# Four edits to the opening of a float32 attention and two-MLP kernel: order of the weight conversion, form of the shift pass, place of the second block's state products, order of the attention's PSUM banks

## The chip, the cores and the metric

The kernel runs on one core of a Trainium2 chip. The metric is the time of one execution on the device, in microseconds (us), the median of several runs. TensorE is called PE here (its weight loads PEld), VectorE DVE, ScalarE ACT, GpSimd POOL; SP is the engine that issues nearly all DMAs.

## The reference

Inputs are `x` (8 x 8 heads x 512 x 64), `state` (8 x 8 x 32 x 64) and two MLPs' weights, which arrive as float64.

```
scores = x @ state^T / 8 ; a = softmax(scores) ; xread = a @ state
scores2 = state @ x^T / 8 ; a2 = softmax(scores2) ; sread = a2 @ x
z = heads joined of [xread, sread]              # 8 x 544 rows of 512
h = z @ w1_in (512 x 2048) ; g = max(h,0) + alpha*min(h,0) ; y = g @ w1_out (2048 x 512)
h2 = y @ w2_in ; g2 = h2 - tanh(h2) ; out = g2 @ w2_out
```

## The kernel before

**Precision.** Each float32 operand is split into a high part (rounded to fp32r, PE's input format) and a low part (the rest); a product is three matmuls, `TERMS` (line 29): high x high, high x low, low x high.

**Weight conversion.** The float64 words of the first MLP's weights become high and low parts in 32 jobs (list `jobs`, line 127): job (f, 0) makes slice f (128 columns) of `w1_in`, called an input slice here, job (f, 1) slice f (128 rows) of `w1_out`, an output slice. A job goes through a pipeline, one stage a tick: `conv_load` (a DMA of 512 KB on SP's queue), `conv_a` (ACT, absolute value), `conv_b` (DVE, `high_word`: a clamp, line 115, and the shift pass, line 117, which shifts left by 3 and masks), `conv_s` (DVE, `sign_word`, line 120; ACT, low word), `conv_c` (ACT copy of the high part; POOL add, line 167), `conv_d` (POOL subtract, lines 173 and 176). `high_word` also serves the second MLP's weights, 32 times, in `combine` (tiles named `c_m`), in the middle of the span.

**Order of the work.** An order written out by hand. The MLP's work is a list of visits (block, slice f): block 0 with slices 0 to 7, block 1 with all 16, block 0 with 8 to 15, then the other blocks. A visit issues `emit_h` (the input product, line 605: 12 matmuls in block 0, 6 in block 1), `act_a` (ACT line 612, DVE 613, ACT 614), `act_b` (DVE 618, low part of the activations) and `emit_o` of the visit before (the output product, line 633, 12 matmuls). Between them are five places, early, gap, mid, late and end; `at(block, slice, place, step)` hangs a step there. `halves` hangs the conversion's ticks, two a visit in block 0's first half and one in block 1, but two in block 1's slices 2 to 4. Every engine does its instructions in the order of issue, so a step that waits holds up all that is behind it on its engine.

**Attention.** The next block's attention is done in steps `s0` to `s6` between the MLP's products. Its PSUM tiles come from the pool `ps_a`, two banks used by turns: a new tile waits until the tile two back has been read. The transposes of the state (`state_turn`, line 361) and the state products (below) take banks of the same pool.

**State products.** From block 1 on the attention's read is not computed first: `project_one(b, q, g, p)` (line 403) multiplies the state with 512 columns q of `w1_in` (line 410, three matmuls), for a pair of heads p of half g, and `emit_h` uses the result `PW` with the attention weights. Rows 0 to 63 and 64 to 127 of one product belong to two blocks (1 and 2 here). Before, high and low part go to a staging tile (lines 413 and 414; for block 1 free parts of a weight tile first, the attention's buffers later), from there to DRAM (line 416), and `load_parts` (line 418) brings block 1's rows back into `PW` (line 423; in the first two quarters slots of the tile `wo`, later buffers `raw`).

**First loads.** `load_x` and `load_state` fetch the first block's first half on SP's queue and its second half on ACT's (`queue`, line 310).

Of the kernel before, what the change touches and what calls it, by code (L numbers as in the profile page):

```python
# [12 lines left out]
F32 = mybir.dt.float32  # L13
F32R = mybir.dt.float32r
I32 = mybir.dt.int32
# [7 lines left out]
P = 128  # L23
# [12 lines left out]
def attention_and_two_mlps(ctx, tc, x, state, w1_in, w1_out, alpha, w2_in, w2_out, out):  # L36
# [30 lines left out]
    ident = const.tile([P, P], F32, name="ident")  # L67
    mask = const.tile([P, GH], F32, name="mask")
    par = const.tile([P, 2], F32, name="par")
    alpha_sb = const.tile([P, NF], F32, name="alpha_sb")  # L70

    sign = const.tile([P, NF], F32, name="sign")
# [3 lines left out]
    def setup():  # L76
        make_identity(nc, ident)
        nc.vector.memset(mask, 0.0)
        nc.vector.memset(par, 0.0)
        for h in range(GH):  # L80
            nc.vector.memset(mask[h * NS:(h + 1) * NS, h:h + 1], 1.0)
            nc.vector.memset(par[h * NS:(h + 1) * NS, h % 2:h % 2 + 1], 1.0)
        nc.sync.dma_start(out=alpha_sb, in_=alpha.rearrange("(f p) -> p f", p=P))
# [30 lines left out]
    def high_word(m):  # L114
        nc.vector.tensor_scalar(m.bitcast(F32), m.bitcast(F32), HIGH_MAX, HIGH_MIN,
                                op0=ALU.min, op1=ALU.max)
        nc.vector.tensor_scalar(m, m, 3, LOW30, op0=ALU.logical_shift_left, op1=ALU.bitwise_and)

    def sign_word(m, r):
        nc.vector.scalar_tensor_tensor(m, r[:, :, 1], SIGN_TOP, m,  # L120
# [3 lines left out]
        nc.scalar.activation(q, r[:, :, 0].bitcast(U32), AF.Copy, scale=2.0**-29)  # L124


    jobs = [(f, half) for f in range(NF // 2) for half in range(2)]
    jobs += [(f, 0) for f in range(8, 12)] + [(8, 1)] + [(f, 0) for f in range(12, 16)] + [(f, 1) for f in range(9, NF)]
    raws, words, low, loaded = {}, {}, {}, set()

    def conv_load(k):
# [175 lines left out]

    xraw, SG = {}, {}

    def queue(b, g):  # L310
        return nc.scalar if (b, g) == (0, 1) else nc.sync

    def load_state(b, g, tag="sg"):
        sg = work.tile([P, D], F32, tag=tag, name=f"{tag}{b}_{g}", bufs=4)
        queue(b, g).dma_start(out=sg, in_=state[b, g * GH:(g + 1) * GH].rearrange("h n d -> (h n) d"))
        SG[(b, g) if tag == "sg" else (b, g, 0)] = sg

    def load_x(b, g):
        if b < 2:
            load_state(b, g)  # L320
        if b == 0:
            if g == 0:
                xraw[b] = w_outs.tile([P, 2 * NC * GH * D], F32, tag="wo", name="xr0")
            n = NC * GH * D
            t = xraw[b][:, g * n:(g + 1) * n].rearrange("p (c h d) -> p c h d", c=NC, h=GH)
        else:
            t = work.tile([P, NC, GH, D], F32, tag="xr", name=f"xr{b}_{g}")
        for h in range(GH):
            queue(b, g).dma_start(out=t[:, :, h, :],
                              in_=x[b, g * GH + h].rearrange("(p c) d -> p c d", c=NC))  # L330
        xraw[b, g] = t

# [40 lines left out]
            nc.vector.tensor_tensor(o[:, 1, sel, :], src, o[:, 0, sel, :].bitcast(F32), op=ALU.subtract)  # L373

    def parts_tile(b, q, g):
        if b == 1 and q < 2:
            open_wo(NF // FQ - 1)
            t = WO[NF // FQ - 1][:, :, 2 * q + g, :]
        else:
            t = work.tile([P, 2, DM], F32R, tag="raw", name="pw", bufs=4)  # L380
        PW[b, q, g] = [t[:, 0], t[:, 1]]
        return t
# [5 lines left out]
    def staged(b):  # L388


        if b > 1:
            return (work.tile([P, DM], F32R, tag="cm", name="ph", bufs=3),
                    work.tile([P, DM], F32R, tag="cq", name="pl", bufs=3))
        k = n_staged[0]
        n_staged[0] += 1
        if k < 8:
            open_wi(NF // FQ - 1)
            return tuple(WI[NF // FQ - 1][:, i, k % NCC, :] for i in range(2))
        return tuple(work.tile([P, DM], F32R, tag=t, name="pe", bufs=1) for t in (("e2", "e2t"), ("sc", "at"))[k % 2])
# [3 lines left out]
    def project_one(b, q, g, p):  # L403


        both = b + 1 < B
        cols, d = (slice(2 * p, 2 * p + 2), slice(0, P)) if both else (slice(3 * p, 3 * p + 1), slice(p * HP, (p + 1) * HP))
        ps = ps_a.tile([P, DM], F32, tag="a", name="ps_p")[:P if both else HP]
        for k, (i, j) in enumerate(TERMS):
            nc.tensor.matmul(ps, lhsT=SN[b, g][:, i, cols, :].rearrange("p k m -> p (k m)"),  # L410
                             rhs=WI[q][:, j, g * NP + p, :], start=(k == 0), stop=(k == 2))
        hi, lo = staged(b)
        nc.scalar.copy(hi[d], ps)
        nc.vector.tensor_tensor(lo[d], ps, hi[d].bitcast(F32), op=ALU.subtract)
        for k, t in enumerate((hi, lo)):
            nc.sync.dma_start(out=pw_dram[b, q, g][p, k, d], in_=t[d].bitcast(F32))

# [614 lines left out]
    def at(i, f, when, *todo):  # L1032
        plan.setdefault((i, f, when), []).extend(todo)

    def timetable(i, a, c):

        if i == 0:
            when = dict(s0=(2, "late"), s1=(3, "early"), s2=(3, "late"), s2t=(3, "end"), s2b=(3, "end"), s3=(3, "end"),
                        s3x=(4, "gap"), s3b=(4, "late"), s4=(4, "end"), s4m=(4, "end"), s4t=(4, "end"), s4b=(5, "gap"),
                        s5=(5, "early"), s6=6)  # L1040
            then = dict(s0=(5, "late"), s1=(6, "early"), s2=6, s2t=(6, "late"), s2b=(6, "late"), s3=(6, "late"),
                        s3x=(6, "end"), s3b=7, s4=(7, "early"), s4m=(7, "early"), s4t=(7, "gap"), s4b=7, s5=(7, "late"),
                        s6=(NF, "late"))
        else:
            def table(first):
                return dict(s0=first, s1=first + 1, s2=first + 2, s2t=(first + 3, "gap"), s2b=first + 3,
                            s3=(first + 4, "gap"), s3x=first + 4, s3b=(first + 4, "late"), s4=(first + 5, "gap"),
                            s4m=first + 5, s4t=(first + 6, "gap"), s4b=(first + 6, "late"), s5=first + 6,
                            s6=(first + 7, "late"))
            start = 7 if i + 2 < B else 5  # L1050
            when, then = (table(0), table(start)) if i > 1 else (table(9), table(8 + NF))
        for g, table in ((a, when), (c, then)):
            for name, w in table.items():
                f, place = w if isinstance(w, tuple) else (w, "mid")

                if f >= NF:
                    j, f = (1, f - NF) if i == 0 else (0, f - NF + (NF // 2 if g is a else 0))
                    at(j, f, place, getattr(g, name))
                else:
                    at(i, f, place, getattr(g, name))  # L1060

    with tc.manual_schedule():
# [15 lines left out]

        for f in range(NF // 2):
            halves(0, f, "early", "gap")  # L1080
        for f in range(11):
            if f in (2, 3, 4):
                halves(1, f, "early", "gap", "mid", "end")
            else:
                halves(1, f, "gap", "end")
        at(0, 0, "gap", a.s2b)
        at(0, 0, "late", c.s2b)
        at(0, 1, "mid", a.s3b, c.s3b)
        at(0, 2, "mid", a.s5)
        at(0, 2, "late", c.s5)  # L1090
        at(0, 3, "mid", a.s6, c.s6)
        a = attention(1, 0)
        turns = [(0, 1, 0, (0, "mid"), (1, "late")), (0, 2, 0, (1, "late"), (2, "early")),
                 (0, 1, 1, (3, "mid"), (4, "early")), (0, 2, 1, (3, "late"), (4, "late"))]
        for i in (2, 4, 6):
            turns += [(i, i + 1, 0, (0, "early"), (0, "late")), (i, i + 1, 1, (2, "late"), (3, "late"))]
            if i + 2 < B:
# [13 lines left out]
            at(i, f, "early", partial(state_mask, b, g, True))  # L1111
            at(i, f, "end", partial(state_turn, b, g, scores=False))
        todo = [(1, q, g) for q in range(NF // FQ) for g in range(NG)]
        places = [(0, 4), (0, 5), (1, 0), (1, 1), (1, 3), (1, 4), (1, 6), (1, 7)]
        todo += [(b, q, g) for b in (3, 5, 7) for g in range(NG) for q in range(NF // FQ)]
        places += [(0, f) for f in range(8, NF)] + [(2, f) for f in range(NF)]
        for (b, q, g), (i, f) in zip(todo, places):
# [1 line left out]
            at(i, f, "late", partial(project_one, b, q, g, 1))  # L1119
        for k in range(2 * NF // FQ):  # L1120
            at(*((0, 9 + 2 * k) if k < 4 else (2, 2 * k - 7)), "end", partial(save_w_in, k // 2, k % 2))
        for q, (i, f, place) in enumerate(((0, 7, "early"), (1, 2, "late"), (1, 6, "early"), (1, 9, "early"))):
            at(i, f, place, partial(load_parts, 1, q))
        at(0, 10, "late", load_half_sum)
        for i, (blk, n) in enumerate(seq):
            if 1 < blk < B:
# [4 lines left out]
        for i, (blk, n) in enumerate(seq):  # L1131
            if i + 1 < B:
                timetable(i, a, attention(i + 1, 1))
                if i + 2 < B:
                    a = attention(i + 2, 0)
                    for j, f in (((1, 2), (1, 4)), ((0, 9), (0, 15)))[i] if i < 2 else ((i, 6), (i, 13)):
                        at(j, f, "late", load_next_x)
            if i + 1 < len(seq) and seq[i + 1][0] == B:
                nn = seq[i + 1][1]
                at(i, 13, "mid", partial(load_reads, nn))  # L1140
                for cc in range(NCC):
                    at(i, *((NF - 1, "early") if cc > 1 else (14, "mid")), partial(split_reads, cc, nn))
# [184 lines left out]
```

## Time and profile before

| | us |
|---|---|
| median of 3 runs | 1507.78 (1504.39 to 1513.72) |
| the profiled execution, whole | 1510.44 |
| its span, first to last instruction | 1508.6 |
| PE busy in the span | 1422.1 (94%) |
| DVE busy | 991.6 (66%) |
| ACT busy | 729.7 (48%) |
| POOL busy | 532.1 (35%) |
| granted PE clock, mean | 0.982 |

The profile is of one execution. Busy time is the union of an engine's instructions. The whole time has 1.8 us beside the span. The granted clock is the share of PE's full speed, 2.4 GHz, that was given; its other level is 1.2 GHz. PE is nearly always busy from about 180 us on; in the first 180 us it is not, and there DVE is.

### The profile page before, as it was taken

What the parts mean: (1) busy time and instruction counts of PE and PEld (TensorE: products, weight loads), DVE (VectorE), ACT (ScalarE), POOL (GpSimd) and SP (SyncE); (2) the same over time, 40 slices, a digit from 0 to 9 for tenths busy, and PEclk for the clock granted to TensorE, in tenths of its full rate; (3) what the DMA queues carried; (4) which work ended last, traced back from release to release, by engine and by line L of the source; (5) the groups of instructions that cost most, each with busy time, mean ns of one, the idle gap of its engine ahead of it and who ended that gap; (6) DMA issues with size and microseconds to landing.
All of it is one profiled execution on the core that took longest, in us unless ns stands there. A gap on an engine that the chain in (4) does not pass through costs nothing. (4 is left out here: it accounts for less than half of the span.)

```text
span 1508.6 us, 22873 instructions
## 1 busy us (share of the span) xinstructions
PE 1422.1 (94%) x8188; PEld 1192.1 (79%) x8188; DVE 991.6 (66%) x1430; ACT 729.7 (48%) x1322; POOL 532.1 (35%) x414
## 2 busy tenths in 40 slices
PE   5868899999899999999999899999999999999998
PEld 2656687677677677778887787887988999999998
DVE  6879855556577667676345555646347798788874
ACT  3656543444565555555334444545345444444443
POOL 2545400000254444445200222212016486666662
PEclk9998999999999999999999999999999999999999
DMA  5458628795688587749864666272795834444321
GB/s 150 137 163 253 206 80 286 268 300 129 188 213 238 156 247 225 239 158 298 237 209 151 253 202 247 103 272 105 276 346 205 324 133 141 133 141 140 133 85 36
DMA packets 230979, 294.41 MB, mean 195 GB/s; under 512 B 57809, under 2 KB 133585, under 8 KB 229841
## 3 DMA queue, kind: packets, MB, share of 16 engines
q1 hardware_dynamic: 228608, 292.39, 60.2%
q8 instruction: 64, 1.05, 0.3%
q10 hardware_dynamic: 2256, 0.56, 0.2%
q14 instruction: 51, 0.41, 0.1%
HBM read 170.73 MB, written 122.16 MB: 194 GB/s over the span
## 5 line engine op out<-in xcount | busy, mean ns | idle before, releaser
L633 PE MATMUL acc<-g,wo 128*128 128x512 f32 (+1 forms) x1728 | 416.2, 388 | 20.8 <-ACT g L614 11.8
L633 PEld LDWEIGHTS acc<-g,wo 128*128 128x128 f32 x1728 | 312.2, 191 | 104.0 <-ACT g L614 16.6
L1001 PE MATMUL ps_m<-wp,s 128*128 128x256 f32 x2856 | 343.5, 283 | 2.1 <-ACT e L984 2.0
L1001 PEld LDWEIGHTS ps_m<-wp,s 128*128 128x128 f32 x2856 | 342.5, 191 | 3.2 <-ACT e L984 2.2
L820 PE MATMUL ps_m<-x,ch 128*128 128x512 f32 x1344 | 312.7, 394 | 8.6 <-DVE c L837 4.5
L820 PEld LDWEIGHTS ps_m<-x,ch 128*128 128x128 f32 x1344 | 251.7, 188 | 69.0 <-DVE c L837 6.5
L946 DVE TENSOR_TENSOR s<-gt,s 128x512 fp32r<-128x512 f32 (+1 forms) x216 | 220.5, 1072 | 45.4 <-ACT s L962 44.4
L613 DVE SCALAR_TENSOR_TENSOR ps_h<-ps_h,sign,t 128x512 f32<-128x512 f32 (+1 forms) x144 | 104.7, 727 | 144.9 <-ACT t L612 144.4
L614 ACT ACTIVATE g<-ps_h,sign 128x512 fp32r<-128x512 f32 (+1 forms) x144 | 95.8, 666 | 160.5 <-DVE ps_h L613 160.5
L962 ACT CAST s<-gt 128x512 fp32r<-128x512 f32 (+1 forms) x216 | 120.3, 597 | 90.9 <-PE ps_m L1001 37.5
L605 PE MATMUL ps_h<-x,pw 128*128 128x512 f32 x624 | 162.7, 396 | 0.9 <-DMA pw<-pw 0.9
L618 DVE SCALAR_TENSOR_TENSOR g<-ps_h,sign,g 128x512 fp32r<-128x512 f32 (+1 forms) x144 | 102.6, 713 | 62.1 <-ACT g L614 58.9
L612 ACT ACTIVATE t<-ps_h,slope 128x512 f32<-128x512 f32 (+1 forms) x144 | 95.7, 664 | 88.3 <-PE ps_h L605 88.0
L605 PEld LDWEIGHTS ps_h<-x,pw 128*128 128x128 f32 x624 | 114.4, 188 | 26.1 <-issue 1.3
L237 POOL TENSOR_TENSOR c_q<-c_m,c_q 128x512 int32<-128x512 int32 x32 | 42.2, 1319 | 262.3 <-ACT c_q L124 213.0
L831 POOL TENSOR_TENSOR t<-c,t 128x512 f32<-128x512 f32 x32 | 41.7, 1303 | 252.1 <-ACT t L830 239.9
L830 ACT ACTIVATE t<-c 128x512 f32<-128x512 f32 x96 | 60.5, 632 | 123.2 <-DVE c L837 110.3
L837 DVE TENSOR_TENSOR c<-ps_m,c 128x512 f32<-128x512 f32 x96 | 64.7, 685 | 58.9 <-PE ps_m L820 43.2
L264 POOL TENSOR_TENSOR c_o<-c_q,c_o 128x512 fp32r<-128x512 f32 (+1 forms) x48 | 54.4, 1134 | 109.6 <-ACT c_o L262 109.6
L831 DVE TENSOR_TENSOR t<-c,t 128x512 f32<-128x512 f32 x64 | 53.9, 843 | 46.6 <-ACT t L830 46.6
L928 POOL TENSOR_TENSOR s<-gt,gt 128x512 f32<-128x512 f32 (+1 forms) x36 | 53.5, 1492 | 83.2 <-DMA gt<-g 81.5
L167 POOL TENSOR_TENSOR cq<-cm,cq 128x512 int32<-128x512 int32 x32 | 42.0, 1313 | 95.7 <-DVE cm L120 60.5
(138 smaller groups left out, 1663.0 us busy)
## 6 DMA issues: line engine op xcount, KB each, us to landing
g<-t SPq DMA_DIRECT2D x128, 256.0 KB, 2.3
gt<-g SPq DMA_DIRECT2D x64, 512.0 KB, 4.9
wc<-c_o SPq DMA_DIRECT2D x112, 256.0 KB, 3.4
ch<-wc SPq DMA_DIRECT2D x56, 512.0 KB, 7.6
pw<-pw SPq DMA_DIRECT2D x104, 256.0 KB, 5.1
wp<-wc SPq DMA_DIRECT2D x28, 512.0 KB, 7.6
raw<-in_moe_w_in SPq DMA_DIRECT2D x16, 512.0 KB, 4.6
raw<-in_moe_w_out SPq DMA_DIRECT2D x16, 512.0 KB, 4.8
```

The source lines that it names most:

```text
L605: nc.tensor.matmul(ps[:, :n], lhsT=w[i], rhs=xt[:, j, :n], start=(k == 0 and m == 0), stop=(k == len(pairs) - 1 and m == 2))
L612: nc.scalar.mul(t, ph, slope[:, f:f + 1])
L613: nc.vector.scalar_tensor_tensor(ph, ph, sign[:, f:f + 1], t, op0=ALU.mult, op1=ALU.max)
L614: nc.scalar.mul(g[:, 0, :n], ph, sign[:, f:f + 1])
L618: nc.vector.scalar_tensor_tensor(g[:, 1, :n], ph, sign[:, f:f + 1], g[:, 0, :n].bitcast(F32), op0=ALU.mult, op1=ALU.subtract)
L633: nc.tensor.matmul(acc[t][:, :n], lhsT=w[i][:, t * P:(t + 1) * P], rhs=g[:, j, :n], start=(first and k == 0), stop=(last and k == 2))
L820: nc.tensor.matmul(b, lhsT=w[p][:, cc], rhs=XT[key, i][cc][:, q], start=(i not in GOES_ON and cc == k == 0), stop=(cc == 1 and k == 2), sk ...
L831: eng.tensor_tensor(t, h, t, op=ALU.subtract)
L837: nc.vector.tensor_tensor(h, ps[j, i], h, op=ALU.add)
L946: nc.vector.tensor_tensor(made[k - 1][:, 1], src, made[k - 1][:, 0].bitcast(F32), op=ALU.subtract)
L962: nc.scalar.copy(made[k][:, 0], source(blk, i, jj))
L1001: nc.tensor.matmul(dst[:, t * HW:(t + 1) * HW], lhsT=s[:, p, r, t * P:(t + 1) * P], rhs=w[:, q], start=first, stop=(jj == NJ // 2 - 1 and ...
```

## The change

The conversion jobs are reordered, so that input slice f + 1 comes before output slice f, and the last output slices are done in the order 14, 15, 12, 13; of the 14 ticks in block 1 (before: slices 0 to 10, two each at 2, 3 and 4) two each now stand at slices 5 and 12, none at 10 and 11, one at 13. The shift pass becomes an instruction with a tensor as second operand: a one-element column that holds the mask, read again for all 512 columns. The second block's state products with p = 0 are written straight into `PW`; only the half of the rows that is the other block's goes to DRAM, and the half of p = 1 that belongs to block 1 is copied into `PW` by a DMA on the chip. `load_parts` is no longer called for block 1. The first loads are all on SP's queue. Steps that take banks of `ps_a` in block 0's first half, two steps of the third block's attention and two loads of `x` move to other places.

```
+    low30 = const.tile([P, 1], I32, name="low30")
+        nc.vector.memset(low30, LOW30)
...
-        nc.vector.tensor_scalar(m, m, 3, LOW30, op0=ALU.logical_shift_left, op1=ALU.bitwise_and)
+        nc.vector.scalar_tensor_tensor(m, m, 3, low30.to_broadcast([P, DM]), op0=ALU.logical_shift_left, op1=ALU.bitwise_and)
...
-    jobs = [(f, half) for f in range(NF // 2) for half in range(2)]
-    jobs += [(f, 0) for f in range(8, 12)] + [(8, 1)] + [(f, 0) for f in range(12, 16)] + [(f, 1) for f in range(9, NF)]
+    jobs = [(0, 0)] + [j for f in range(1, NF // 2) for j in ((f, 0), (f - 1, 1))] + [(7, 1)]
+    jobs += [(f, 0) for f in range(8, 12)] + [(8, 1)] + [(f, 0) for f in range(12, 16)] + [(f, 1) for f in (9, 10, 11, 14, 15, 12, 13)]
...
-    def queue(b, g):
-        return nc.scalar if (b, g) == (0, 1) else nc.sync
...
-        if b == 1 and q < 2:
+        if b == 1 and q < 3:
             open_wo(NF // FQ - 1)
-            t = WO[NF // FQ - 1][:, :, 2 * q + g, :]
+            t = WO[NF // FQ - 1][:, :, 2 * (q % 2) + g, :]
...
-        if k < 8:
+        if k < 4:
...
-        hi, lo = staged(b)
+        if b == 1 and p == 0:
+            parts_tile(b, q, g)
+            hi, lo = PW[b, q, g]
+        else:
+            hi, lo = staged(b)
         nc.scalar.copy(hi[d], ps)
         nc.vector.tensor_tensor(lo[d], ps, hi[d].bitcast(F32), op=ALU.subtract)
+        if b == 1:
+            e = slice((1 - p) * HP, (2 - p) * HP)
+            for k, t in enumerate((hi, lo)):
+                nc.sync.dma_start(out=pw_dram[b, q, g][p, k, e], in_=t[e].bitcast(F32))
+            if p:
+                for k, t in enumerate((hi, lo)):
+                    nc.sync.dma_start(out=PW[b, q, g][k][HP:].bitcast(F32), in_=t[HP:].bitcast(F32))
+            return
...
-            when = dict(s0=(2, "late"), s1=(3, "early"), s2=(3, "late"), s2t=(3, "end"), s2b=(3, "end"), s3=(3, "end"),
+            when = dict(s0=(3, "early"), s1=(3, "gap"), s2=(3, "late"), s2t=(3, "end"), s2b=(3, "end"), s3=(3, "end"),
...
-                        s3x=(6, "end"), s3b=7, s4=(7, "early"), s4m=(7, "early"), s4t=(7, "gap"), s4b=7, s5=(7, "late"),
+                        s3x=(6, "end"), s3b=(7, "early"), s4=(7, "early"), s4m=(7, "early"), s4t=(7, "gap"), s4b=7, s5=(7, "late"),
...
-            when, then = (table(0), table(start)) if i > 1 else (table(9), table(8 + NF))
+            when, then = (table(0), table(start)) if i > 1 else ({**table(9), "s0": (10, "early"), "s1": (10, "late")}, table(8 + NF))
...
-        for f in range(11):
-            if f in (2, 3, 4):
+        for f in (*range(10), 12, 13):
+            if f in (5, 12):
                 halves(1, f, "early", "gap", "mid", "end")
...
-        at(0, 1, "mid", a.s3b, c.s3b)
+        at(0, 1, "mid", a.s3b)
+        at(0, 1, "late", c.s3b)
...
-        turns = [(0, 1, 0, (0, "mid"), (1, "late")), (0, 2, 0, (1, "late"), (2, "early")),
-                 (0, 1, 1, (3, "mid"), (4, "early")), (0, 2, 1, (3, "late"), (4, "late"))]
+        turns = [(0, 1, 0, (0, "mid"), (2, "early")), (0, 2, 0, (1, "late"), (2, "gap")),
+                 (0, 1, 1, (3, "mid"), (4, "early")), (0, 2, 1, (3, "late"), (4, "mid"))]
...
-        places = [(0, 4), (0, 5), (1, 0), (1, 1), (1, 3), (1, 4), (1, 6), (1, 7)]
+        places = [(0, 5), (0, 6), (1, 0), (1, 1), (1, 4), (1, 5), (1, 8), (1, 9)]
...
-        for q, (i, f, place) in enumerate(((0, 7, "early"), (1, 2, "late"), (1, 6, "early"), (1, 9, "early"))):
-            at(i, f, place, partial(load_parts, 1, q))
...
-                    for j, f in (((1, 2), (1, 4)), ((0, 9), (0, 15)))[i] if i < 2 else ((i, 6), (i, 13)):
+                    for j, f in (((1, 4), (1, 10)), ((0, 9), (0, 15)))[i] if i < 2 else ((i, 6), (i, 13)):
```

## Rows read from the trace of the kernel before

**Rows 1.** Busy time by stretch: start:end, length, each engine, clock, DMA share, GB/s
```profile
181.00:209.00 28.00, 28.00 (x157) 21.87 (x156) 16.56 (x31) 12.32 (x23) 1.96 (x2) 1.00 0.07 19
...
390.00:715.00 325.00, 308.20 (x1644) 240.93 (x1642) 225.03 (x378) 182.57 (x331) 154.68 (x150) 0.99 0.73 215
715.00:1508.60 793.60, 776.02 (x4920) 701.10 (x4920) 504.06 (x604) 354.16 (x640) 291.24 (x195) 0.99 0.54 185
```

**Rows 2.** Waits of PE, 20 to 190 us: us in total, times, longest
```profile
PE ps_h L605 <- DMA wo<-pw: 5.2, 4, 3.9
PE ps_xt L460 <- DVE wi L414: 4.1, 1, 4.1
PE ps_r L558 <- ACT e2t L530: 3.9, 1, 3.9
PE ps_h L605 <- POOL wi L173: 3.5, 1, 3.5
PE ps_p L410 <- DVE wi L414: 3.2, 1, 3.2
...
PE ps_st L361 <- ACT e2t L530: 2.2, 1, 2.2
```

**Rows 3.** Busy time by stretch, cut at starts of DVE's line 613
```profile
36.60:118.20 81.60, 61.90 (x362) 45.55 (x363) 65.78 (x120) 49.87 (x95) 41.41 (x32) 0.89 0.50 150
118.20:183.40 65.20, 56.05 (x229) 43.09 (x228) 59.62 (x76) 41.37 (x73) 35.83 (x27) 0.93 0.84 254
```

**Rows 4.** The same, single visits
```profile
36.60:44.70 8.10, 6.85 (x27) 5.59 (x28) 7.76 (x14) 6.20 (x12) 5.51 (x5) 0.79 0.76 223
...
73.30:87.20 13.90, 9.63 (x72) 7.07 (x70) 11.03 (x22) 7.06 (x15) 5.90 (x5) 1.00 0.50 164
87.20:99.50 12.30, 7.52 (x28) 5.43 (x28) 6.30 (x13) 7.33 (x13) 5.60 (x4) 0.72 0.54 172
...
140.10:148.80 8.70, 5.63 (x14) 4.03 (x15) 8.59 (x12) 5.72 (x10) 5.58 (x5) 0.61 1.03 233
...
155.60:160.00 4.40, 2.50 (x12) 1.73 (x11) 4.37 (x6) 2.90 (x5) 2.72 (x2) 1.00 0.94 273
```

**Rows 5.** DVE by line, 29.4 to 181 us: count, busy us, mean ns, idle before
```profile
L117 DVE TENSOR_SCALAR cm<-cm 128x512 int32<-128x512 int32 x30 | 28.4, 947 | 1.0
L120 DVE SCALAR_TENSOR_TENSOR cm<-raw,cm 128x512 int32<-128x512 int32 x30 | 23.1, 772 | 0.3
L115 DVE TENSOR_SCALAR cm<-cm 128x512 f32<-128x512 f32 x29 | 19.4, 670 | 0.3 <-ACT cm L112 0.3
```

**Rows 6.** Single DVE lines, whole span: ns min/median/max, first and last start
```profile
L117 DVE TENSOR_SCALAR c_m<-c_m x32: 426/428/1501, 391.2 to 712.3; 128x512 int32<-128x512 int32 x32
L543 DVE TENSOR_TENSOR sc<-sc,sm x16: 674/682/1576, 19.6 to 668.7; 128x512 f32<-128x512 f32 x16
```

**Rows 7.** DVE in order of time: start, us, instruction
```profile
131.27 1.40 DVE L117 TENSOR_SCALAR cm<-cm 128x512 int32<-128x512 int32 x1
...
133.25 1.11 DVE L120 SCALAR_TENSOR_TENSOR cm<-raw,cm 128x512 int32<-128x512 int32 x1
```

**Rows 8.** POOL in order of time, the same stretch
```profile
131.04 1.35 POOL L167 TENSOR_TENSOR cq<-cm,cq 128x512 int32<-128x512 int32 x1 [2.89 <-DVE cm L120]
132.34 1.48 POOL L176 TENSOR_TENSOR wo<-cq,wo 128x512 fp32r<-128x512 f32 x1
```

**Rows 9.** DMA issues by kind, 60 to 181 us: count, KB each, median us to landing
```profile
pw<-wi SPq DMA_DIRECT2D x16, 256.0 KB, 2.1
...
wo<-pw SPq DMA_DIRECT2D x8, 256.0 KB, 6.5
```

**Rows 10.** PE in order of time, first 16 us
```profile
6.66 1.09 PE L460 MATMUL ps_xt<-ident,xr 128*128 128x128 f32 x4 [2.56 <-DMA xr<-in_x]
...
12.80 1.91 PE L460 MATMUL ps_xt<-ident,xr 128*128 128x128 f32 x8
```

**Rows 11.** SP's queue in order of time, first 16 us
```profile
1.21 2.88 SPq L329 DMA_DIRECT2D xr<-in_x  x4
```

More of the change, by code (lines that the diff above doesn't have):

```diff
@@ L308, in attention_and_two_mlps @@
     xraw, SG = {}, {}
-    def queue(b, g):
-        return nc.scalar if (b, g) == (0, 1) else nc.sync
     def load_state(b, g, tag="sg"):
         sg = work.tile([P, D], F32, tag=tag, name=f"{tag}{b}_{g}", bufs=4)
-        queue(b, g).dma_start(out=sg, in_=state[b, g * GH:(g + 1) * GH].rearrange("h n d -> (h n) d"))
+        nc.sync.dma_start(out=sg, in_=state[b, g * GH:(g + 1) * GH].rearrange("h n d -> (h n) d"))
         SG[(b, g) if tag == "sg" else (b, g, 0)] = sg
@@ L328, in load_x @@
         for h in range(GH):
-            queue(b, g).dma_start(out=t[:, :, h, :],
+            nc.sync.dma_start(out=t[:, :, h, :],
                               in_=x[b, g * GH + h].rearrange("(p c) d -> p c d", c=NC))
```

## The prediction

> **What bounds the kernel.** I first read the busy time by stretch. From 715 us PE is busy 776.0 of 793.6 us, from 390 to 715 us 308.2 of 325, and already from 181 to 209 us all 28 of 28 [rows 1]: there the edits can give next to nothing, since they take no work from PE. What can be won lies before 181 us. The waits of PE there are the second view: the largest that the edits touch are 5.2 us for the state products' way back from DRAM, 4.1 and 3.2 us for DVE's line 414 (a state product holds a bank), 3.9 and 2.2 us for the copy of `e2t` (again a bank), and 3.5 us for POOL's conversion of an input slice [rows 2]. That is 22 us, and it would be the gain if PE set the pace. The third view speaks against that. Cut at line 613, which each visit needs once, the stretch 36.6 to 118.2 us (block 0's eight visits) has 65.8 us of DVE in 81.6, and 118.2 to 183.4 us (block 1's first ten) has 59.6 in 65.2, while PE has 61.9 and 56.1 [rows 3]. DVE's idle time is 15.8 and 5.6 us. A wait of PE that falls while DVE is full anyway is worth nothing when it goes; so I make the sum on DVE: its work, plus what idle time remains.
>
> **Shift pass.** Now it takes 428 ns when free and up to 1501 [rows 6], 947 on average in the opening [rows 5]. The long ones run beside POOL: one began at 131.27 us and lasted 1.40, to 132.67; POOL's first addition had ended at 132.39 [rows 7, 8]. Line 120, with two operands in SBUF, does the same: begun at 133.25, it ended at 134.36, 0.54 after POOL's next operation [rows 7, 8]. So two SBUF operands do not get it past POOL. The nearest row to the new form is line 543, two SBUF operands of which the second is read with repeats: 682 ns free, 1576 at most [rows 6]. I take +0.25 us (682 - 428) for each shift, free or waiting. The 30 shifts from 29.4 to 181 us cost 7.7; of these 16 stand in block 0's visits (+4.1), 11 in block 1's first ten (+2.8), and some 5 before 36.6 us, where DVE has no gaps either (+1.3). The bounds: -7.9, if the mask does not count as an operand from SBUF and no shift waits (30 x (682 - 947)), to +7.7. In `combine` 32 shifts are worth +8.1 of DVE, which has 100 us free of 325 [rows 1]; the cover is that free time, PE idles 16.8 us there, and I charge 1 (bounds 0 and 8.1).
>
> The Trainium skill (SBUF — State Buffer, Who interferes with whom) says that a DVE instruction with two SBUF inputs contends with a POOL instruction that reads SBUF, and that one with at most one SBUF input outside the two-port modes does not. The rows on line 120 agree with the first half; whether a repeated one-element column counts as an input no row shows, and by the second half, if it does not, the sum would be that of rival B.
>
> **Ticks.** Block 1's first ten visits lose two of 13 ticks. A tick of DVE is 0.67 + 0.95 + 0.77 = 2.4 us [rows 5], so -4.8. They go to slices 12 and 13, where DVE has 11 us free [rows 1]. There POOL becomes late: two ticks in one visit are four operations of about 1.4 us [rows 8], 5.7 us, against a visit of 28/6 = 4.7; the output product of slice 12 waits for the last but the input product stands before it: +0.7 (bounds 0 and 2). The new order of the last slices has no other cost: 12 and 13 are overwritten after their last reader, slice 11.
>
> **An input slice ahead.** The 3.5 us wait goes, but DVE had 7.76 busy in the 8.10 us of that visit [rows 4]: it gives 0.3. Output slices come one tick later and still a visit before their use; POOL's work is the same.
>
> **Banks.** In the visit of 13.9 us DVE idles 2.9, nearly all behind the state products that move a visit later: -2.4. In that of 12.3 it idles 6.0, at a granted clock of 0.72, part of it at 1.2 GHz [rows 4]. The transposes behind line 414 keep their place there, since another product stands where one stood; I give this visit -2.8 for DVE arriving earlier and the clock. The wait of 2.2 us for `e2t` in slices 1 to 2 goes for 1.8, as `s3b` and the state's transpose no longer share the moment. The 3.9 us before slice 7's end I value at 1.5, since a state product's way back is removed behind it and DVE has two ticks to do. The products newly in slice 6 put a bank wait before `s2`: +0.8. Together with the 0.3 above: -8.0. Were this DVE time filled otherwise, it would be 0.
>
> **State products.** The eight pairs of products need 48 transfers as before (32 writes, 16 reads or copies), so SP issues as many; each has 128 KB instead of 256 [rows 9], in all 6.3 MB instead of 12.6. The landing took 2.1 us for a write in an empty queue and 6.5 for a read back in a full one [rows 9]; the copy that replaces it lies between (I take 4, nearer the reads), and two visits of 4.4 us or more cover it. SP waits for line 414 and for the first half's write before it issues the copy; behind it stand the next raw weights, needed two ticks later. If it is late, the 3.9 us come back. The wait itself fell in a visit in which DVE was busy 8.59 of 8.70 us [rows 4], so that removing it is worth little by itself: DVE's 59.6 become 59.6 - 4.8 + 2.8 = 57.6, and of 5.6 idle I leave 1.0, since visits with one tick and no product run at 4.40 with 4.37 busy [rows 4]. So 58.6 instead of 65.2: -6.6.
>
> **First loads.** The second half's four loads go behind the first half's on SP, some 2.9 us for four [rows 11]. The first half lands at 6.66, the second half is first needed at 12.80 [rows 10]; about 3.3 us later than now it would land near 10. The raw weights, 3.3 us later too, are used only after this part of the attention. Cost 0, bounds -1 and +1. The moved loads of `x` and steps of the third block fall in the stretch where DVE and ACT are half idle: 0.
>
> **Sum.** Before 36.6: +1.3. Block 0: +4.1 - 8.0. Block 1: -6.6. Behind: +0.7 + 1. Total -7.5, from 1510.4 of the profiled execution to 1502.9. That execution lies 2.7 above the median of 1507.8; against the median the forecast is **1500**.
>
> **Rivals.**
> A, the forecast, with its own range 1492 to 1508: 47%.
> B, the mask is no second operand: the shift passes POOL. Instead of +8.2 in the opening there is -7.9, of which I count half, since line 120 comes next and takes over a part of the waits: 8.2 + 4 = 12 below A, 1488. For it: the mask is one element. Against: line 543's long ones. 22%.
> C, DVE was the whole bound: the gaps reappear elsewhere and banks and products give 2 instead of 8; or the copy on the chip is late, so that what is called kept on the chip still waits. 1506 to 1508. For it: 59.6 of 65.2; against: gaps of 6 us in one visit. 20%.
> D, slower: the longer shift is on the path wherever it stands, 8.2 in the opening and 8.1 in `combine`, 16 us: 1524. It decides if DVE sets the pace in `combine` as well; against it stand DVE's 225 of 325 us there. 11%.
>
> **Chances.** A measurement of this kernel tells about 1% from no change, that is 1492.7 and 1522.9. Below lie a quarter of A and nine tenths of B: 0.32. Above lies some 0.6 of D: 0.07. Within: 0.61. The range leaves out a bit of B's low end and most of D: 1484 to 1514.
>
> **What would show it.** Line 117's successor at 680 ns with a tail of 1.6 us (A) or a flat 690 (B). No wait of PE for the products' DMA at slices 0 and 4 of block 1, and none for POOL's line 173 at slice 1. Line 613 of block 1's slice 10 at about 174 us (183.4 - 9.2) instead of 183.4 if I am right, with DVE over 95% busy from 118 us on. If in the new profile PE has over 19 of 20 us before 150 us, DVE was not the bound and I am wrong.

## The result and the profile after

The changed kernel took **1523.3 us** (median; 1519.3 to 1526.3) beside 1508.6 for the kernel before on the same chip: a ratio of 1.0092, with an interval from 1.0073 to 1.0112. It is slower by a little under 1%; the forecast was 1500, the range ended at 1514, and 0.07 stood on slower. Its profiled execution took 1525.6, with a span of 1523.8 against 1508.6, so the two traces differ by 15.2 us.

Busy time, page of the changed kernel, the first of its parts:

```profile
PE 1428.2 (94%) x8188; PEld 1192.7 (78%) x8188; DVE 1006.8 (66%) x1431; ACT 729.7 (48%) x1322; POOL 540.1 (35%) x414
```

PE has 6 us more, DVE 15. The next view is busy time by stretch (columns as in [rows 1]); the first three lines answer to [rows 1], the others are cut at starts of the line that was 613 (625 now, DVE's step once a visit): block 0's eight visits and block 1's first ten (both answer to [rows 3]), slice 6 of block 0 alone, and the 70 visits in which `combine` converts the second MLP's weights.

```profile
181.00:209.00 28.00, 25.91 (x116) 19.45 (x115) 20.06 (x34) 15.43 (x30) 9.01 (x7) 1.00 0.36 81
390.00:715.00 325.00, 305.71 (x1554) 233.97 (x1554) 225.47 (x365) 175.07 (x316) 146.64 (x140) 0.98 0.71 208
715.00:1523.80 808.80, 789.27 (x5051) 713.37 (x5049) 515.58 (x622) 364.47 (x661) 304.90 (x205) 1.00 0.55 188
...
35.60:128.50 92.90, 64.99 (x355) 47.12 (x356) 70.98 (x121) 49.48 (x95) 43.06 (x31) 0.83 0.40 113
128.50:192.40 63.90, 55.81 (x226) 42.52 (x225) 57.33 (x75) 39.44 (x70) 31.83 (x24) 0.95 0.62 173
100.30:121.30 21.00, 15.42 (x82) 10.33 (x82) 11.66 (x21) 7.60 (x14) 5.23 (x4) 0.84 0.41 113
387.30:732.40 345.10, 324.75 (x1700) 252.14 (x1699) 238.21 (x385) 187.40 (x340) 157.90 (x151) 0.98 0.73 214
```

The same 70 visits in the kernel before:

```profile
378.30:717.00 338.70, 321.77 (x1709) 251.37 (x1708) 229.54 (x384) 187.34 (x340) 156.52 (x152) 0.99 0.74 218
```

The account by these cuts: 1.0 us gained before the first visit, **+11.3 in block 0's eight visits**, -1.3 in block 1's first ten, nothing from there to `combine` (194.9 us both times), **+6.4 in `combine`**, -0.2 behind it. Within block 0 one visit holds nearly all of the loss: slice 6 takes 21.0 us, where it took 10.3. Slices 2 and 3 lose another 4.2, and slices 4, 5 and 7 give 3.3 back (table of visits below). In slice 6 DVE is busy 11.7 us and PE 15.4, at a granted clock of 0.84; neither is full. The same visit in the kernel before:

```profile
99.50:109.80 10.30, 9.46 (x44) 7.07 (x40) 9.93 (x18) 6.07 (x11) 5.08 (x4) 1.00 0.37 105
```

The waits of PE in the changed kernel, 20 to 190 us, with one line of the stretch up to 220 us below (columns as in [rows 2]):

```profile
PE ps_e L540 <- ACT e L522: 5.2, 2, 4.4
PE ps_r L570 <- DVE snp L372: 4.7, 1, 4.7
PE ps_p L409 <- DVE wide L580: 4.2, 1, 4.2
PE ps_s L506 <- DVE wo L417: 4.0, 1, 4.0
PE ps_xt L472 <- DVE wo L417: 3.4, 1, 3.4
...
PE acc L645 <- POOL wo L178: 0.9, 1, 0.9
```

The waits for DRAM and for POOL's input slice [rows 2] are gone, as the edits meant; in their place stand bank waits of the same size, one of them at `s2` of slice 6 (4.0 us, behind DVE's line 417, which was 414).

DVE by line, 29 to 183 us (answers to [rows 5]; the shift pass is line 119 now), and the shift pass alone over the whole span, in the first MLP's weights and the second's (answers to [rows 6]):

```profile
L119 DVE SCALAR_TENSOR_TENSOR cm<-cm,low 128x512 int32<-128x512 int32 x27 | 32.4, 1199 | 0.9
L122 DVE SCALAR_TENSOR_TENSOR cm<-raw,cm 128x512 int32<-128x512 int32 x26 | 19.3, 741 | 0.2
L117 DVE TENSOR_SCALAR cm<-cm 128x512 f32<-128x512 f32 x27 | 18.5, 686 | 0.0
...
L119 DVE SCALAR_TENSOR_TENSOR cm<-cm,low x32: 691/694/1801, 19.8 to 200.9; 128x512 int32<-128x512 int32 x32
L119 DVE SCALAR_TENSOR_TENSOR c_m<-c_m,low x32: 691/693/1756, 400.7 to 727.6; 128x512 int32<-128x512 int32 x32
```

A free shift went from 428 to 693 ns, the mean in the opening from 947 to 1199: +0.25 us either way, and the long ones are still there.

### The profile page after: what moved, and what is told of

It is laid out like the page before. It is cut to its first block, busy times and chain, and to the rows that moved or that the text cites. A ratio compares the mean times of both kernels' runs of the same rounds, so it can differ in the third digit from the quotient of the medians.

```text
span 1523.8 us, 22862 instructions
## 1 busy us (share of the span) xinstructions
PE 1428.2 (94%) x8188; PEld 1192.7 (78%) x8188; DVE 1006.8 (66%) x1431; ACT 729.7 (48%) x1322; POOL 540.1 (35%) x414
## 4 chain that ended last, share of the span: by engine, by line
PE 63%; DVE 9%; DMA 6%; ACT 5%; issue 4%; POOL 1%; SPq 1%; DVEq 0%; ACTq 0%; POOLq 0%
PE ps_m L1013 20%; PE ps_m L832 17%; PE acc L645 13%; PE ps_h L617 8%; DVE ps_h L625 2%; PE ps_p L409 2%; DVE g L630 2%; PE ps_m L897 2%; ACT g L626 1%; ACT t L624 1%; DMA c_raw<-in_moe_w_in 1%; DVE c_m L119 1%; DMA pw<-pw 1%; DMA wc<-c_o 1%; DMA gt<-g 1%
## 5 line engine op out<-in xcount | busy, mean ns | idle before, releaser
L645 PE MATMUL acc<-g,wo 128*128 128x512 f32 (+1 forms) x1728 | 428.1, 396 | 27.4 <-ACT g L626 17.8
L645 PEld LDWEIGHTS acc<-g,wo 128*128 128x128 f32 x1728 | 318.3, 195 | 116.3 <-ACT g L626 23.0
L1013 PEld LDWEIGHTS ps_m<-wp,s 128*128 128x128 f32 x2856 | 338.5, 190 | 4.9 <-ACT e L996 3.3
L617 PE MATMUL ps_h<-x,pw 128*128 128x512 f32 x600 | 156.5, 396 | 0.0
L239 POOL TENSOR_TENSOR c_q<-c_m,c_q 128x512 int32<-128x512 int32 x32 | 42.1, 1315 | 252.4 <-ACT c_q L126 194.1
L617 PEld LDWEIGHTS ps_h<-x,pw 128*128 128x128 f32 x600 | 110.6, 189 | 24.2
```

Source lines behind the costliest of these rows:

```text
L617: nc.tensor.matmul(ps[:, :n], lhsT=w[i], rhs=xt[:, j, :n], start=(k == 0 and m == 0), stop=(k == len(pairs) - 1 and m == 2))
L645: nc.tensor.matmul(acc[t][:, :n], lhsT=w[i][:, t * P:(t + 1) * P], rhs=g[:, j, :n], start=(first and k == 0), stop=(last and k == 2))
L1013: nc.tensor.matmul(dst[:, t * HW:(t + 1) * HW], lhsT=s[:, p, r, t * P:(t + 1) * P], rhs=w[:, q], start=first, stop=(jj == NJ // 2 - 1 and ...
```

## The experiments

The runs were made in three sets (`e1` to `e4`, `e5` to `e8`, `e9` to `e11`); the kernel before ran in each, with medians of 1510.5, 1510.9 and 1510.2. The ratios against it, with 95% intervals, are the recorded estimates; they differ from the quotient of the two medians by up to 0.0012.

| run | median us | ratio (interval) |
|---|---|---|
| `e1_plain_shift` | 1512.5 | 1.0008 (0.9995 to 1.0020) |
| `e2_shift_alone` | 1519.7 | 1.0062 (1.0044 to 1.0080) |
| `e3_slice6_end` | 1516.5 | 1.0028 (1.0014 to 1.0042) |
| `e4_slice6_plain` | 1505.5 | 0.9957 (0.9942 to 0.9973) |
| `e5_shift_second_mlp` | 1514.3 | 1.0022 (1.0008 to 1.0035) |
| `e6_banks_undone` | 1501.6 | 0.9940 (0.9922 to 0.9957) |
| `e7_old_job_order` | 1508.1 | 0.9975 (0.9962 to 0.9988) |
| `e8_queue_alone` | 1506.6 | 0.9973 (0.9962 to 0.9984) |
| `e9_second_at_end` | 1511.5 | 1.0003 (0.9991 to 1.0016) |
| `e10_slices_5_6_end` | 1502.2 | 0.9949 (0.9934 to 0.9964) |
| `e11_through_dram` | 1508.5 | 0.9991 (0.9980 to 1.0003) |

Lengths of block 0's eight visits, slices 0 to 7, from the starts of the line once 613 in each trace (us):

| | 0 | 1 | 2 | 3 | 4 | 5 | 6 | 7 |
|---|---|---|---|---|---|---|---|---|
| before | 8.1 | 9.0 | 9.0 | 10.7 | 13.8 | 12.3 | 10.3 | 8.4 |
| after | 8.3 | 8.5 | 10.5 | 13.4 | 12.3 | 11.7 | 21.0 | 7.2 |
| `e1_plain_shift` | 8.1 | 8.0 | 11.4 | 11.8 | 11.7 | 11.7 | 20.4 | 6.9 |
| `e9_second_at_end` | 8.2 | 8.0 | 11.4 | 11.8 | 11.7 | 11.6 | 17.7 | 6.9 |
| `e3_slice6_end` | 8.4 | 8.5 | 11.4 | 11.8 | 12.3 | 12.9 | 12.2 | 7.2 |
| `e4_slice6_plain` | 8.1 | 8.0 | 11.5 | 11.8 | 11.7 | 11.7 | 12.0 | 6.9 |
| `e6_banks_undone` | 8.1 | 8.2 | 9.0 | 10.7 | 11.7 | 11.8 | 12.0 | 7.5 |

**The shift pass.** Taken out of the changed kernel (`e1_plain_shift`), put alone into the kernel before (`e2_shift_alone`), and alone there in `combine` only (`e5_shift_second_mlp`, where `high_word` gets a flag that `combine` sets).

```diff
 e1 (against after)
-  nc.vector.scalar_tensor_tensor(m, m, 3, low30.to_broadcast([P, DM]), ...)
+  nc.vector.tensor_scalar(m, m, 3, LOW30, ...)
 e2 (against before): the same two lines, the other way round
 e5 (against e2)
-    def high_word(m):
+    def high_word(m, wide=False):    # the new form if wide, else the old one
-            high_word(m[h])
+            high_word(m[h], True)    # in combine
```

> The changed kernel with the old shift pass (an immediate as mask), all else as changed. Theory 1: of the 15 us lost, some 9 to 10 come from the state products that now stand in block 0's slice 6, and some 6 from the longer shift pass, nearly all of it between 390 and 715 us, where the second MLP's weights are converted. Then this kernel takes 1514 to 1517 us, the visits of block 0 from slice 6 to 7 still take some 20 us, and the drift from 390 to 715 us is gone. Theory 2: the shift pass is the whole loss, since DVE is full in the opening and sets the pace there too. Then it takes 1508 or less and the visit of slice 6 shrinks with it.

> The kernel before with the new shift pass alone. Theory 1: about 6 us slower from 390 to 715 us and 0 to 4 in the opening, 1514 to 1519 in all. Theory 2: the whole loss, 1522 to 1525. A third view, that the shift pass costs nothing and the drift after 390 us comes from other timing, gives 1508.

> The kernel before with the new shift pass only where the second MLP's weights are converted (390 to 715 us); the first MLP's conversion keeps the old one. Theory 1: DVE's 25 to 30% of free time there does not cover the 8 us more, because it lies in waits for ACT inside each visit, while the shift stands ahead of line 613 and puts it off; so 3 to 6 us slower than before, and the opening as before. Theory 2, my forecast's: the free time covers it, 0 to 1 us slower.

All three say that the longer shift costs time: 0.6% alone, 0.8% in the changed kernel (1.0092 to 1.0008), 0.2% for `combine` alone. The stretch of the 70 visits in `combine`, in the three traces (`e1_plain_shift`, then `e2_shift_alone`, then `e5_shift_second_mlp`):

```profile
381.70:718.90 337.20, 320.25 (x1697) 249.86 (x1696) 228.72 (x384) 187.35 (x340) 155.02 (x151) 0.99 0.74 218
```

```profile
381.80:724.20 342.40, 323.51 (x1701) 250.91 (x1700) 238.12 (x385) 187.41 (x340) 157.53 (x151) 0.99 0.74 215
```

```profile
379.20:724.20 345.00, 323.48 (x1701) 251.18 (x1700) 238.19 (x384) 187.20 (x340) 157.35 (x151) 0.99 0.74 214
```

Against 338.7 before, the new form adds 3.7 and 6.3 us where it was put in, and taking it out of the changed kernel gives 7.9 back (345.1 to 337.2). DVE has over 100 us free in the stretch in all of them. The same 70 visits can be read in every trace of this case: 336.5 to 338.9 us in the nine kernels with the old form, 342.4 to 346.2 in the four with the new one, 6.7 between the means. The 32 shifts take some 9 us more in all (28.6 to 29.1 against 19.3 to 19.7), so about three quarters of that get through. How this happens, the kernel before shows in order of time:

```profile
395.92 0.43 DVE L117 TENSOR_SCALAR c_m<-c_m 128x512 int32<-128x512 int32 x1
396.38 0.69 DVE L120 SCALAR_TENSOR_TENSOR c_m<-c_raw,c_m 128x512 int32<-128x512 int32 x1
396.99 0.75 DVE L613 SCALAR_TENSOR_TENSOR ps_h<-ps_h,sign,t 128x512 f32<-128x512 f32 x1
```

The conversion runs back to back into line 613, the step that a visit's output product waits for. DVE's free time stands between other instructions, as waits for ACT, and a longer shift in front of line 613 can't use it. The traces bear this out: added up over the 70 visits, line 613 begins 35.3 to 37.2 us after the end of ACT's line 612, which it needs, in the nine kernels with the old form, and 42.1 to 42.5 in the four with the new one. (`e2_shift_alone` was profiled in an execution of 1516.3, 3.4 below its median, `e5_shift_second_mlp` in one 1.8 above its own.)

In the opening `e2_shift_alone` adds 0.2 before the first visit, 0.5 in block 0 and 2.8 in block 1's ten visits. The trace of `e5_shift_second_mlp`, whose first MLP is converted as in the kernel before, has -0.8, +0.3 and +1.8 there, so a difference of 2 us between two single traces says little. In the changed kernel the two forms differ by 5.3 us at the 25th visit (block 0's slice 8, called visit 24 below; 222.5 against 217.2), and with slice 6's products at the end by 5.0 (213.0 against 208.0). So the opening's share is 3.5 to 5.3 us in these traces, and with the share of `combine` it comes near the 9 us that the median of `e2_shift_alone` adds.

**The state products of slice 6.** Both go to the end of the visit (`e3_slice6_end`); that with the old shift (`e4_slice6_plain`); with the old shift, only the second of them (`e9_second_at_end`).

```diff
 e3 (against after)
-  at(i, f, "mid", partial(project_one, b, q, g, 0))
-  at(i, f, "late", partial(project_one, b, q, g, 1))
+  late = (i, f) == (0, 6)
+  at(i, f, "end" if late else "mid", partial(project_one, b, q, g, 0))
+  at(i, f, "end" if late else "late", partial(project_one, b, q, g, 1))
 e4 (against e3): the shift as in e1
 e9 (against e1)
-  at(i, f, "late", partial(project_one, b, q, g, 1))
+  at(i, f, "end" if (i, f) == (0, 6) else "late", partial(project_one, b, q, g, 1))
```

> The changed kernel, but the two state products of block 0's slice 6 are issued at the end of the visit, behind the output product and the attention's score steps, instead of around them. Theory 1: the wait of 4.0 us of the scores for the products' bank and the 8.2 us in which DVE stood behind the second product go, the visit from slice 6 to 7 falls from 21 to 11 or 12 us, total 1513 to 1516. Theory 2: DVE is full, so the gap reappears elsewhere: 1520 to 1524.

> Both at once: the products of slice 6 at the end of the visit, and the old shift pass. Theory 1: the two losses add up, so 1505 to 1510. Theory 2: as with the old shift pass alone, 1508. If 1500 or less, the rest of the change is worth what was forecast without the shift.

> The changed kernel with the old shift pass, and of slice 6's two products only the second at the visit's end; the first stays ahead of the scores. Of the 7 us that both at the end were worth: if DVE's 8.2 us behind the second product are the loss, this kernel comes to 1505 to 1507 (0.996 to 0.997 of before); if the 4.0 us wait of the scores for the first product's bank is, it stays at 1511 to 1513 (1.000).

Moving both gives 0.64% with the new shift (1.0092 to 1.0028) and 0.51% with the old (1.0008 to 0.9957); slice 6 falls to 12.2 and 12.0 us. Moving only the second gives nothing that the medians tell (1.0003), though slice 6 falls to 17.7 in its trace. So it is the first that costs most. PE in order of time in the changed kernel (start, us, instruction, and in brackets the idle time before it), then DVE, same stretch:

```profile
98.81 0.94 PE L409 MATMUL ps_p<-wi,snp 128*128 128x512 f32 x3
99.73 0.33 PE L595 MATMUL ps_w<-ident,wide 128*128 128x128 f32 x1
104.10 1.12 PE L506 MATMUL ps_s<-e,stt 128*64 128x512 f32 x1 [4.04 <-DVE wo L417]
...
106.00 5.06 PE L645 MATMUL acc<-g,wo 128*128 128x512 f32 x12
110.90 0.86 PE L409 MATMUL ps_p<-wi,snp 128*128 128x512 f32 x3
```

```profile
103.35 0.69 DVE L417 TENSOR_TENSOR wo<-ps_p,wo 128x512 fp32r<-128x512 f32 x1 [0.79 <-ACT wo L416]
103.96 0.28 DVE L598 TENSOR_REDUCE xw<-ps_w 128x64 f32<-128x128 f32 x1
112.42 0.69 DVE L417 TENSOR_TENSOR wi<-ps_p,wi 128x512 fp32r<-128x512 f32 x1 [8.18 <-ACT wi L416]
113.02 0.71 DVE L512 STREAM_TRANSPOSE sc<-ps_s 128x512 f32<-128x512 f32 x1
```

The first product is done at 99.7, but line 417 reads its bank only at 103.35 to 104.04, since on ACT and DVE the visit's activations and parts of a conversion job stand ahead of it. The scores (506) need a bank and PE stands still for 4.04 us. Then the output product takes 5.06 us for its 12 matmuls. The second product comes behind it on PE, and DVE, whose next instruction in order is that product's subtraction, stands for 8.18 us with the scores' own steps queued behind it: they could have begun at 106 and begin at 113. With both products at the end (`e4_slice6_plain`) PE has no such wait and the same 12 matmuls take 3.02 us:

```profile
96.55 0.64 PE L504 MATMUL ps_s<-e,stt 128*64 128x512 f32 x1 [0.56 <-ACT e2t L475]
...
97.56 3.02 PE L643 MATMUL acc<-g,wo 128*128 128x512 f32 x12
100.42 0.86 PE L407 MATMUL ps_p<-wi,snp 128*128 128x512 f32 x3
```

With only the second at the end (`e9_second_at_end`) the wait and the long product stay, and DVE's wait for a copy of the product is 3.4 us instead of 8.2:

```profile
100.73 1.11 PE L504 MATMUL ps_s<-e,stt 128*64 128x512 f32 x1 [4.05 <-DVE wo L415]
...
102.63 5.00 PE L643 MATMUL acc<-g,wo 128*128 128x512 f32 x12
```

**The order of the banks.** `e4_slice6_plain` with the bank edit undone (`e6_banks_undone`), and that with slice 5's products at the end of their visit as well (`e10_slices_5_6_end`).

```diff
 e6 (against e4): the old places of s0, s1 (slices 2, 3), s3b (1 and 7) and the state's turns
-  s0=(3, "early"), s1=(3, "gap")
+  s0=(2, "late"), s1=(3, "early")
-  s3b=(7, "early")
+  s3b=7
-  at(0, 1, "mid", a.s3b)
-  at(0, 1, "late", c.s3b)
+  at(0, 1, "mid", a.s3b, c.s3b)
-  turns = [(0, 1, 0, (0, "mid"), (2, "early")), (0, 2, 0, (1, "late"), (2, "gap")), ...
+  turns = [(0, 1, 0, (0, "mid"), (1, "late")), (0, 2, 0, (1, "late"), (2, "early")), ...
 e10 (against e6)
-  late = (i, f) == (0, 6)
+  late = (i, f) in ((0, 5), (0, 6))
```

> The kernel with the slice-6 products at the visit's end and the old shift pass, and besides the bank edit undone: the state's transposes, s0, s1 and the two s3b stand where they stood before. Theory 1: the bank edit gives little, since a new wait came (s5 4.7 us for the transpose's subtraction in slice 2) for the one that went; within 2 us of the same kernel with the edit, 0.995 to 0.998 of before. Theory 2: the edit is worth the 4 to 6 us that I gave it, then 1.000 of before. Theory 3: it costs, then 0.993 or less.

> The kernel with slice 6's products at the visit's end, the old shift pass and the old bank order, and also slice 5's products at their visit's end. There PE still waits 3.6 us for DVE's wide and 4.1 us for line 414's successor. Theory 1: a product costs by what stands behind it on PE and DVE, so 2 to 4 us less than with slice 6 alone: 1498 to 1500, 0.992 of before. Theory 2: DVE is full in slice 5 as it lags there already, so the same 0.994.

The edit shows no gain: without it the kernel takes 1501.6 us against 1505.5. The two intervals overlap, so the medians don't settle whether and by how much it hurts; the traces put it at 2.8 us in block 0 (79.1 against 81.9), with slices 2 and 3 at 9.0 and 10.7 again instead of 11.5 and 11.8, less what slice 7 gives back. What goes with the edit is the wait for `snp`, 4.2 us in `e4_slice6_plain` and 4.7 in the table of waits above: a transpose of the state, now at slice 2's start, has its bank read late, and `s5` of the first half stands behind it. The parts of this edit were not tried singly. Moving slice 5's products as well shows no further gain (1502.2).

**The first loads.** All on SP's queue, alone, in the kernel before (`e8_queue_alone`).

```diff
-        return nc.scalar if (b, g) == (0, 1) else nc.sync
+        return nc.sync
```

> The kernel before with all first loads on SP's queue and nothing else. Theory 1: nothing beyond 1 us, as forecast. Theory 2: the 2.4 us by which the kernels with the whole change reach block 0's first visit earlier come from it: line 613 first at 34 us instead of 36.6, and 2 us less in all.

It gives 0.27%. PE and ACT at the start of `e8_queue_alone`, and ACT at the start of the kernel before:

```profile
4.97 1.09 PE L460 MATMUL ps_xt<-ident,xr 128*128 128x128 f32 x4 [0.99 <-DMA xr<-in_x]
```

```profile
0.74 1.28 ACT L484 ACT_TABLE_LOAD   x1 [0.74 <-PEq L1311]
```

```profile
0.73 0.39 ACTq L315 DMA_DIRECT2D sg<-in_state  x1
1.16 2.66 ACTq L329 DMA_DIRECT2D xr<-in_x  x4
3.85 1.28 ACT L484 ACT_TABLE_LOAD   x1 [3.85 <-issue]
```

The first tile of `x` can be transposed at 4.97 us instead of 6.66 [rows 10], although nothing of its own load changed [rows 11]; the second half's loads now come behind it instead of beside it. This holds in all traces: 4.79 to 5.32 us in the ten with one queue, 6.22 to 6.66 in the three with two. And ACT, freed of five issues, loads its table 3.1 us earlier. The first visit then starts at 33.8 instead of 36.6, and 3.2 us of lead are still there at visit 24 (209.5 against 212.7).

**The way on the chip.** `e6_banks_undone` with block 1's products written to DRAM and read back as in the kernel before; the products stay at their new places (`e11_through_dram`).

```diff
 e11 (against e6): the new branch of project_one taken out, staging tiles as before; the reads put back
+  for q, (i, f, place) in enumerate(((0, 7, "early"), (1, 2, "late"), (1, 6, "early"), (1, 9, "end"))):
+      at(i, f, place, partial(load_parts, 1, q))
```

> The kernel with slice 6's products at the visit's end, the old shift pass and the old bank order, but block 1's state products go through DRAM as before (write all, read back), at the changed kernel's visits. Theory 1: the way on the chip by itself is worth little, since DVE sets the pace and the products now stand two visits ahead of use: 0.994 to 0.996 of before. Theory 2: the waits for the read back return with 4 to 5 us: 0.997.

1508.5 against 1502.2 of `e10_slices_5_6_end`, measured beside it, and 1501.6 of `e6_banks_undone`: the way on the chip is worth 6.3 to 6.9 us, a little under half a per cent. PE's first wait from 90 to 200 us in this trace is the one that `e6_banks_undone` doesn't have:

```profile
PE ps_h L602 <- DMA wo<-pw: 6.2, 4, 3.2
```

At visit 24 the two traces lie as far apart, 6.2 us (212.0 and 205.8). As the products come a visit later than in the kernel before, the reads had less time here than there, where the wait was 5.2 [rows 2].

**The order of the jobs.** `e4_slice6_plain` with the old order of the first 16 jobs (`e7_old_job_order`).

```diff
-    jobs = [(0, 0)] + [j for f in range(1, NF // 2) for j in ((f, 0), (f - 1, 1))] + [(7, 1)]
+    jobs = [(f, half) for f in range(NF // 2) for half in range(2)]
```

> The same kernel (slice-6 products at the end, old shift pass) with the first sixteen conversion jobs in the old order, so that the second input slice is converted one job later. Theory 1: DVE is full in the first visits and the 3.5 us wait of PE is worth less than 1 us, so 0.995 to 0.997 of before. Theory 2: the wait is worth its 3.5 us: 0.998 to 0.999.

The median is 0.18% higher with the old order, with intervals that overlap. In the trace block 0's visits take 82.4 instead of 81.9, and at visit 24 the difference is 0.7 us (208.7 against 208.0), although PE's waits for POOL's input slices are back with 3.6 us. What the medians show beyond that arises later, where the edit does nothing; it stays open.

## Why the prediction was wrong

**What held.** The price of a shift: +0.25 was forecast, 0.25 to 0.27 measured (of the 32 shifts of the first MLP 5, 15 and 12 stand in the three stretches, not 5, 16 and 11, which moves 0.3 us). Its place beside POOL is seen here, DVE and POOL of the changed kernel in order of time (answers to [rows 7, 8]):

```profile
60.74 1.65 DVE L119 SCALAR_TENSOR_TENSOR cm<-cm,low 128x512 int32<-128x512 int32 x1
```

```profile
60.51 1.33 POOL L169 TENSOR_TENSOR cq<-cm,cq 128x512 int32<-128x512 int32 x1 [3.41 <-DVE cm L122]
61.80 1.71 POOL L178 TENSOR_TENSOR wo<-cq,wo 128x512 fp32r<-128x512 f32 x1
```

POOL's addition ends at 61.84 and the shift 0.55 later, as line 120 did [rows 7, 8], and not past it. The Trainium skill (SBUF — State Buffer, Who interferes with whom) says that an instruction with two SBUF inputs contends with a POOL instruction that reads SBUF; this trace agrees, and shows that a column of one element read 512 times counts as such an input. So rival B fell. What the exchange lost, the Trainium skill has on another page (VectorE: DVE Perf Modes, What auto-detection actually checks): a single-source instruction with source and destination in SBUF can, under a condition on their sizes, run in a two-port double mode. The rows agree, 428 ns before and 693 with a second source.

The other signs came as named: no wait for the products' DMA at slices 0 and 4, none for POOL at slice 1, the lateness of slice 12 at 0.9 us (forecast 0.7), DVE's work in block 1's ten visits at 57.3 (57.6). An input slice ahead was put at 0.3 for a wait of 3.5 that goes, and `e7_old_job_order` shows 0.7 in its trace. The landing on the chip took less than the 4 us that I took for it (DMA issues 60 to 181 us, writes to DRAM in the first line, copies on the chip in the second; answers to [rows 9]):

```profile
pw<-wo SPq DMA_DIRECT2D x12, 128.0 KB, 2.3
...
wo<-wi SPq DMA_DIRECT2D x8, 128.0 KB, 2.3
```

**The step that failed first: "The products newly in slice 6 put a bank wait before `s2`: +0.8."** I had named the mechanism and priced it as one short wait. It was 10.7 us in the trace (21.0 against 10.3), of which moving both products to the end took 8.8 back (21.0 to 12.2 in `e3_slice6_end`). The price of the bank was the time until its reader came up on its own engine. That was readable before: line 414 already held PE for 4.1 and 3.2 us [rows 2], and I used those rows as gains of the places that the products left, not as prices of the place where they went. I also counted only one of three effects: the wait, PE's slower product behind it, and DVE standing for the second product with the attention behind it.

**The second: the shift in `combine`, "I charge 1 (bounds 0 and 8.1)".** It cost 3.7 to 7.9 us in the pairs of traces above, 6.7 between the means of all of them, and 3.3 in the medians of `e5_shift_second_mlp` (1.2 to 5.3 by its interval): well over 1, and by the traces near the upper bound. The cover that I named, DVE's 100 us of free time, was not where the shift stood. This was rival D's condition and price, and D's 1524 is what came; but its sum is right by chance, since the opening's share of it (8.2) was smaller in the traces (3.5 to 5.3) and slice 6 filled the place.

**The third: the sum of the banks, "Together with the 0.3 above: -8.0."** The terms for products that left slices 4 and 5, -2.4 and -2.8, came in part (13.8 to 11.7, 12.3 to 11.8, in `e6_banks_undone`); the edit of `s0`, `s1`, `s3b` and the state's turns showed no gain and cost about 3 us in the trace. The wait for `e2t` that it took away came back as one for `snp`.

**Two terms too small.** "First loads. ... Cost 0, bounds -1 and +1" measured -4; I asked when the moved half would be needed, and not what it had been delaying. The state products' way was called "worth little by itself" because DVE was busy 8.59 of 8.70 us in that visit [rows 4]; it is worth 6.3 to 6.9. Block 1's slice 3 fell from 8.7 to 3.7 us, and with the products through DRAM (`e11_through_dram`) it takes 8.5.

**The premise beneath.** I made the sum on DVE's idle time, with the forecast that DVE would be over 95% busy from 118 us on. In the changed kernel it is 57.3 of 63.9, that is 90%: DVE did the work that I gave it, but idled 6.6 us where I left 1.0. In block 0's eight visits it is 71.0 of 92.9, and PE, with 65.0, is not full either. Line 613's successor of block 1's slice 10 began at 192.4, not near 174. By stretches the sum said +1.3, -3.9, -6.6 and +1.7 us; the traces have -1.0, +11.3, -1.3 and +6.2. Here the two engines wait for each other by turns, which leaves both part idle, and neither engine's sum is the time. The ticks' -4.8, the new order of the last output slices and the moved steps and loads of the later blocks weren't tried alone.

**What works.** Without the new shift, with slice 6's products at the end and the old bank order (`e6_banks_undone`), the change takes 1501.6 us, 0.9940 (0.9922 to 0.9957): below both kernels, and near the 1500 forecast for other reasons, as the queue (-4) and the way on the chip (-6) pay for it.

## What to carry to other kernels

Price a product put before another user of its bank by where its reader stands in the reading engine's queue, and look up the waits that the same instruction causes elsewhere in the trace. Free time of an engine covers a longer instruction only if it lies between that instruction and the next step that something waits for. Before a two-operand form replaces an immediate, compare the two forms' shortest durations: here the immediate ran in 428 ns and the tensor form in 693, and both waited for POOL.

## What the runs showed of the hardware

Two queues loading at once did not hasten the first tile: with all loads on SP's queue it could be used at 4.97 us instead of 6.66. The Trainium skill (DMA: Bandwidth & Descriptors, Issuing engines are not separate DMA queues) says that issuing from several engines saves only the time of the issue; the run agrees, in that the second queue brought no gain, and shows a loss of 1.7 us besides.

An idle PE can cost twice: in slice 6, after the wait of 4.04 us, the next 12 matmuls took 5.06 us; after a wait of 0.56 (`e4_slice6_plain`) they took 3.02. It need not: in slice 3 a wait of 2.76 us was followed by 12 matmuls in 4.58 us in the changed kernel and in 3.00 in `e4_slice6_plain`. The granted clock was 0.84 over slice 6 of the changed kernel, so part of it was at 1.2 GHz, and 1.00 over the same visit of `e4_slice6_plain`:

```profile
97.10:109.20 12.10, 11.48 (x78) 8.51 (x78) 11.28 (x21) 7.63 (x14) 5.08 (x4) 1.00 0.67 174
```
